# Chunked attention into a swish MLP on one core: the first two units' q and k transposed on TensorE instead of VectorE

## The chip, the core and the metric

The kernel runs on one core of a Trainium2 chip. Time is device time in microseconds (us) of one execution; lower is better. PE is TensorE (PEld its weight loads), DVE is VectorE, ACT is ScalarE, POOL is GpSimd, SP is SyncE. SBUF is the on-chip working memory, PSUM the eight banks that TensorE writes its results to.

## What is computed

Attention inside chunks of 64 tokens for 8 x 8 heads, then a two-layer MLP whose activation is h * sigmoid(beta * h):

```
q, k, v: (8, 8, 576, 64) float32        # batch, head, token, head_dim
scores = (q_chunk @ k_chunk.T) / 8      # 64 x 64 for each chunk and head
attn   = softmax(scores)
x      = (attn @ v_chunk) -> (4608, 512)
h      = x @ w_in                       # w_in (512, 2048)
out    = (h * sigmoid(beta * h)) @ w_out   # w_out (2048, 512), out (4608, 512) float32
```

## The kernel before

**Tiling.** The 4608 tokens are 18 units of 256 (four chunks, two tiles of 128 tokens, called s = 0 and s = 1). Two units make a block of 512 tokens. For a unit, the q and k rows are transposed so that the head dimension lies on the partitions; `emit_sc` writes the transposed scores into PSUM, ACT takes the exponential into `et`, `emit_pv` multiplies `et` with v (a column of ones beside v gives the sums), `emit_norm` divides on DVE and writes `x16`, and the result is transposed into `xt` (the products' right operand). For a block, `emit_m(j, m)` makes 128 rows of h (four matmuls), a tanh on ACT (`act`) and one DVE instruction (`vec`) that frees the product's PSUM bank and writes `gt`; `emit_t` multiplies `gt` with w_out, and ACT copies out.

**Order.** Everything is issued in the order of the code (`manual_schedule`), each engine in its own order. The part around the change is the start, written out by hand, before the first block's products run without a break. What waits there is filled on PE by matmuls whose result nobody reads (`emit_tiny`, `emit_idle`); one of them (L425) waits for a memset of `late` that stands in POOL's queue.

**Loads at the start.** SP loads q and k of heads 0 to 3 in float32 (`raw`), POOL loads heads 4 to 7 with a cast to float16 (`h`), both for 512 tokens with token 4p + r on partition p. Then POOL issues v of tiles 0 to 3 (`load_v`), writes the identity, and issues the eight pieces of w_in and the first of w_out. All of POOL's loads go through one queue.

**Units 0 and 1.** `emit_T_half(a)` handles four heads: for a = 0 ACT casts `raw` to float16 in 1 + 2 pieces, and DVE transposes q and k in 32 x 32 blocks, each pair of float16 values taken as one float32 word. The scores (`emit_sc_half`, L198) are therefore matmuls over 32 partitions, two (e = 0, 1) accumulated for each 64 x 64 result. The order that follows is: scores (0,0), exponential, scores (0,1), exponential, scores (1,0), `emit_pv(0)`, scores (1,1), the exponential of unit 1 in one piece, the two norms of unit 0, the transposes of `x16` of (0,0), `emit_pv(1)` for both tiles, the norms of (1,1) and (1,0), and then the products m = 0 to 3 over unit 0's 256 tokens with the remaining transposes between them:

```
d[0][0]()
emit_xt_pe(1, 1)
d[1][0]()
d.append(emit_m(0, 2, 0, 256, True))
d[0][1]()
emit_xt_pe(1, 0, nc.vector.tensor_copy)
```

`d[i][0]` is the tanh of product i, `d[i][1]` its DVE instruction. After these come products 0 to 3 over unit 1's tokens, then 4 to 15 over all 512. The pool `ps_p` has four PSUM banks, so the fifth product takes the bank of the first. `emit_xt_pe` transposes one 128 x 512 tile of `x16` on PE into PSUM (L303) and copies it to `xt` (L304), on ACT or, for (1,0), on DVE.

**Later.** `emit_T(2)` transposes unit 2 on DVE; its scores stand at position i = 8 of 16 in the first block's second layer, its `emit_pv` at i = 10, and unit 3's scores at i = 14.

Of the kernel before, what the change touches and what calls it, by code (L numbers as in the profile page):

```python
# [8 lines left out]
FP32 = mybir.dt.float32  # L9
FP16 = mybir.dt.float16  # L10
ACTF = mybir.ActivationFunctionType
# [4 lines left out]
def kernel(  # L16
# [10 lines left out]
    nc = tc.nc  # L27
# [5 lines left out]
    KFF = DFF // 128  # L33
    UNIT = 256
# [3 lines left out]
    scale = 1.0 / float(D) ** 0.5  # L38
# [20 lines left out]
    HH = H // 2  # L59
    raw0 = [const.tile([128, HH, 4, D], FP32, name=f"raw{i}") for i in range(2)]  # L60
    qk0 = [[const.tile([128, HH, 4, D], FP16, name=f"h0{i}{a}") for i in range(2)] for a in range(2)]
    qkT0 = [[const.tile([128, HH, 128, 2], FP16, name=f"t0{i}{a}") for i in range(2)] for a in range(2)]
    braw = const.tile([128, 32], FP32)
    gate = const.tile([128, 1], FP16)
    bt = const.tile([128, 32], FP32)
# [45 lines left out]
    def load_v(i):  # L111
        for off, n, b, s in runs(i * 128, 128):
            nc.gpsimd.dma_start(  # L113
                out=vbig[off:off + n, i, :, 0:D],
                in_=v[b, :, s:s + n, :].rearrange("h p d -> p h d"),
            )
# [54 lines left out]
    x16_t = {}  # L171
    xt_t = {}

    def emit_T_half(a):
        for i, h0, h1 in ((0, 0, HH), (1, 0, HH // 2), (1, HH // 2, HH)) if a == 0 else ((0, 0, HH), (1, 0, HH)):
            src = qk0[a][i][:, h0:h1]
            if a == 0:
                nc.scalar.copy(out=src, in_=raw0[i][:, h0:h1])  # L178
            nc.vector.transpose(  # L179
                out=qkT0[a][i][:, h0:h1].rearrange("p h s e -> p (h s e)").bitcast(FP32).rearrange(  # L180
                    "p (h i r) -> p h r i", h=h1 - h0, r=4),
                in_=src.rearrange("p h r d -> p (h r d)").bitcast(FP32).rearrange(
                    "p (h r i) -> p h r i", h=h1 - h0, r=4),
            )

    def emit_sc_half(u, a):
        if a == 0:
            et_t[u] = et_p.tile([128, 2, H, CH], FP16, tag="et", name="et")
            pool, tag = ((ps_s, "s"), (ps_x, "x"))[u]
            x_t["sc", u] = pool.tile([128, 2, H, CH], FP32, tag=tag, name="sc")  # L190
        sc = x_t["sc", u]
        qt, kt = qkT0[a]
        for h in range(HH):
            for e in range(2):
                for s in range(2):
                    p0 = 64 * u + 32 * s
                    for c in range(2):
                        nc.tensor.matmul(  # L198
                            out=sc[64 * c:64 * c + 64, s, HH * a + h, :],
                            lhsT=kt[p0:p0 + 32, h, 64 * c:64 * c + 64, e],  # L200
                            rhs=qt[p0:p0 + 32, h, 64 * c:64 * c + 64, e],
                            start=(e == 0),
                            stop=(e == 1),
                        )

    def emit_ex_half(u, a, n=1):
        hs = slice(HH * a, HH * (a + n))
        nc.scalar.activation(  # L208
            out=et_t[u][:, :, hs], in_=x_t["sc", u][:, :, hs], func=ACTF.Exp, scale=scale)

    ex_t = {}

# [38 lines left out]
        while ex_t[u] and not later:  # L251
            emit_ex(u)

    def emit_pv(u, where=("x", "s")):
        et = et_t.pop(u)
        for s in (1, 0) if u >= MU else (0, 1):
            i = 2 * u + s
            if where[s] == "p":
                x = [ps_p.tile([128, 4, 128], FP32, tag="p", name=f"y{r}") for r in range(2)]
            else:  # L260
                pool = {"x": ps_x, "s": ps_s}[where[s]]
                x = [pool.tile([128, 2, 4, 128], FP32, tag=where[s], name="x")]
            for g in range(4):
                for r in range(2):
                    for c in range(2):
                        nc.tensor.matmul(  # L266
                            out=(x[0][64 * c:64 * c + 64, r, g, 0:D + 1] if len(x) == 1 else
                                 x[r][64 * c:64 * c + 64, g, 0:D + 1]),
                            lhsT=(et[64 * r:64 * r + 64, s, 4 * c + g, :] if u < XU else
                                  et[64 * r:64 * r + 64, g % 2, 4 * s + 2 * c + g // 2, :]),  # L270
                            rhs=vbig[64 * r:64 * r + 64, i, 4 * c + g, 0:D + 1],
                        )
            x_t[u, s] = x
# [23 lines left out]

    def emit_xt_pe(u, s, copy=nc.scalar.copy):
        xf = x16_t.pop((u, s)).rearrange("p r h d -> p (r h d)")
        tag = "s" if u < 2 and (u, s) != (1, 0) else "xp"[s]  # L300
        xp = {"x": ps_x, "s": ps_s, "p": ps_p}[tag].tile([128, 4, 128], FP16, tag=tag, name="xp")
        for g in range(4):
            nc.tensor.transpose(out=xp[:, g, :], in_=xf[:, g * 128:(g + 1) * 128], identity=ident)  # L303
        copy(out=xt_at(u, s), in_=xp)  # L304
# [70 lines left out]
    def idle_bank():  # L375
        return ps_p.tile([128, 512], FP32, tag="p", name="warm")

    def emit_idle(n, w, d=None):
        d = idle_bank() if d is None else d
        for _ in range(n):  # L380
            nc.tensor.matmul(out=d[:, 0:w], lhsT=idle[:, 0:128], rhs=idle[:, 0:w])  # L381

    def emit_tiny(n):
        d = [ps_p.tile([128, 512], FP32, tag="p", name="tiny") for _ in range(2)]
        for i in range(n):
            c = i % 4
            p0, o0 = 32 * c, 64 * (c % 2)
            nc.tensor.matmul(
                out=d[c // 2][o0:o0 + 64, 0:8],
                lhsT=tiny[p0:p0 + 32, :],  # L390
                rhs=tiny[p0:p0 + 32, 0:8],
            )

    with tc.manual_schedule():
# [4 lines left out]
        for a, eng, dst in ((0, nc.sync, raw0), (1, nc.gpsimd, qk0[1])):  # L399
            for i, src in enumerate((q, k)):  # L400
                eng.dma_start(
                    out=dst[i],
                    in_=src[0, HH * a:HH * a + HH, 0:2 * UNIT, :].rearrange("h (p r) d -> p h r d", r=4),
                )
        bv = moe_beta.rearrange("(m w f) -> w m f", w=4, f=32)
        for w in range(4):
            nc.sync.dma_start(out=braw[32 * w:32 * w + KFF, :], in_=bv[w])
        for i in range(4):
            load_v(i)
            if i == 1:  # L410
                nc.gpsimd.memset(late, 0.0)
        nxt[0] = 2
        make_identity(nc, ident)
        for g in range(8):
            load_w_in(g)
        for g in range(3):
            load_w_out(g)
# [1 line left out]
        load_w_out(3)  # L419
        loads_to(3)  # L420

        emit_tiny(78)
        warm = idle_bank()
        emit_idle(3, 512, warm)
        nc.tensor.matmul(out=warm[:, 0:16], lhsT=idle[:, 0:128], rhs=late)  # L425
        emit_idle(8, 512, warm)
        emit_T_half(0)
        emit_sc_half(0, 0)
        emit_ex_half(0, 0)
        warm = idle_bank()  # L430
        emit_idle(6, 512, warm)
        emit_T_half(1)
        nc.vector.transpose(out=bt, in_=braw)
        emit_sc_half(0, 1)
        emit_ex_half(0, 1)
        emit_sc_half(1, 0)
        emit_idle(2, 512, warm)
        loads_to(5)
        emit_pv(0, ("s", "p"))
        emit_sc_half(1, 1)  # L440
        emit_ex_half(1, 0, 2)
        emit_norm(0, 0)
        emit_norm(0, 1)
        emit_idle(1, 512, warm)
        emit_idle(12, 64, warm)
        emit_xt_pe(0, 0)
        emit_pv(1, ("x", "p"))
        emit_norm(1, 1)
        emit_norm(1, 0)
        nc.scalar.activation(out=beta2, in_=bt[:, 0:KFF], func=ACTF.Copy, scale=0.5)  # L450
        emit_xt_pe(0, 1)
        d = [emit_m(0, m, 0, 256, True) for m in (0, 1)]
        d[0][0]()
        emit_xt_pe(1, 1)
        d[1][0]()
        d.append(emit_m(0, 2, 0, 256, True))
        d[0][1]()
        emit_xt_pe(1, 0, nc.vector.tensor_copy)
        d.append(emit_m(0, 3, 0, 256, True))
        for act, _ in d[2:]:  # L460
            act()
        for _, vec in d[1:]:
            vec()
        for m in range(4):
            emit_m(0, m, 256, 256)
# [1 line left out]
            emit_m(0, m)  # L467
        emit_T(2)
        for i in range(16):
            if i == 8:  # L470
                emit_sc(2)
            if i == 10:
                emit_pv(2)
                emit_norm(2, 0)
                emit_norm(2, 1)
                emit_T(3)
            if i == 13:
                emit_xt_pair(2)
            if i == 14:
                emit_sc(3, True)  # L480
            if i == 15:
                a0, v0 = emit_m(1, 0, 0, 256, True)
                a0()
                emit_pv(3)
                emit_norm(3, 0)
                emit_norm(3, 1)
                v0()
                emit_m(1, 1, 0, 256)
            emit_t(0, i % 4, 4 * (i // 4), 4 * (i // 4) + 4)
# [156 lines left out]
```

The softmax here doesn't subtract the row's maximum and nothing guards it: scores larger than these inputs give would overflow.

## Time and profile before

| | us |
|---|---|
| median of 9 runs (lowest, highest) | 287.75 (287.39, 288.11) |
| the profiled execution | 287.58 |
| span of its instructions | 285.7 |
| PE busy in it | 278.8 |
| DVE, ACT, POOL busy | 143.8, 146.2, 95.6 |
| PE busy in the first 17.17 us | 13.87 |

The span runs from the first to the last instruction; the profiled execution has 1.9 us around it. A row of the timeline gives the start, the length, engine, line, operation, output and inputs with shapes, the number of instructions merged into it, and in brackets the engine's idle time just before with what ended it. The length of a matmul counts its way through the array, so a stream is read from the starts.

### The profile page before, as it was taken

The numbers are of one execution on the slowest core, as the hardware profiler recorded it, in microseconds if no ns is written. First come the engines' busy times: TensorE is split into PE (matmuls) and PEld (weight loads), VectorE is DVE, ScalarE is ACT, GpSimd is POOL, SyncE is SP. The second block draws the span as 40 slices with busy tenths as digits, with TensorE's granted clock in tenths as the row PEclk, the third lists the DMA queues.
The fourth block names the chain that finished last, engine by engine and source line by source line (L and its number), as shares of the span: only waits on it lengthen the run. The fifth ranks groups of instructions, "written<-read, shape, count | busy, mean of one in ns | idle before, by whom it ended". The sixth has DMA issues, their size and how long they took to land.

```text
span 285.7 us, 6671 instructions
## 1 busy us (share of the span) xinstructions
PE 278.8 (98%) x2779; PEld 136.1 (48%) x2779; DVE 143.8 (50%) x268; ACT 146.2 (51%) x223; POOL 95.6 (33%) x125
## 2 busy tenths in 40 slices
PE   6999999999999999999999999999999999999995
PEld 3564456544544444444444444444444444444444
DVE  2777444776558453635463536363635463333301
ACT  4477128863567545455454545554545444444411
POOL 8843678498074981248617000000000000000000
PEclk9999999999999999999999999999999999999999
DMA  8999999999999999999999993425311221010012
GB/s 195 176 199 204 182 179 213 207 164 154 206 116 163 184 176 175 157 166 172 187 151 169 160 172 77 102 57 118 81 52 39 73 57 55 37 39 37 37 73 76
DMA packets 141085, 37.40 MB, mean 131 GB/s; under 512 B 128000, under 2 KB 136576, under 8 KB 141056
## 3 DMA queue, kind: packets, MB, share of 16 engines
q0 software_dynamic: 99136, 17.83, 79.8%
q1 hardware_dynamic: 41776, 19.09, 33.3%
q8 instruction: 22, 0.36, 0.5%
q10 hardware_dynamic: 144, 0.07, 0.1%
q14 instruction: 7, 0.06, 0.1%
HBM read 36.71 MB, written 9.44 MB: 162 GB/s over the span
## 4 chain that ended last, share of the span: by engine, by line
PE 94%; ACT 1%; DVE 1%; DMA 1%; issue 1%; DVEq 0%
PE hps L329 44%; PE ops L361 43%; PE x L266 2%; DMA raw<-in_q_dram 1%; PE sc L238 1%; PE ops L602 1%; PE sc L225 1%; DVE t L179 1%; PE y L266 1%; ACT xt L304 1%; PE xp L303 0%; PE sc L198 0%; ACT h L178 0%; ACT et L208 0%; PE warm L381 0%
## 5 line engine op out<-in xcount | busy, mean ns | idle before, releaser
L343 DVE SCALAR_TENSOR_TENSOR gt<-sg,hps 128x512 f16<-128x512 f32 (+1 forms) x153 | 99.2, 655 | 102.1 <-ACT sg L339 101.6
L329 PE MATMUL hps<-xt,win 128*128 128x512 f16 (+1 forms) x612 | 136.2, 367 | 1.0 <-ACT xt L304 0.7
L339 ACT ACTIVATE sg<-hps,beta 128x512 f32<-128x512 f32 (+1 forms) x153 | 100.3, 662 | 71.6 <-PE hps L329 70.0
L361 PE MATMUL ops<-wout,gt 128*128 128x512 f16 x560 | 131.1, 380 | 0.0
L329 PEld LDWEIGHTS <-win 128*128 128x128 f16 x612 | 58.1, 98 | 62.9 <-issue 1.5
L361 PEld LDWEIGHTS <-gt 128*128 128x128 f16 x560 | 54.1, 98 | 64.1
L371 ACT ACTIVATE osb<-ops 128x512 f32<-128x512 f32 x35 | 20.9, 598 | 42.7 <-PE ops L361 42.7
L113 POOL DMA_DIRECT2D vbig<-in_v_dram x40 | 34.0, 867 | 11.8 <-DMA wout<-in_moe_w_out_dram 3.7
L99 POOL DMA_DIRECT2D qu<-in_q_dram x22 | 18.7, 860 | 24.4 <-DMA qT<-qu 21.6
L287 DVE TENSOR_TENSOR x<-x,rd 128x512 f16<-128x512 f32 x27 | 18.7, 692 | 1.0
L99 POOL DMA_DIRECT2D ku<-in_k_dram x22 | 18.8, 876 | 0.6 <-DMA ku<-in_k_dram 0.3
L285 DVE RECIPROCAL rd<-x 128x8 f32<-128x8 f32 x27 | 5.4, 200 | 11.4 <-PE x L266 11.4
L247 ACT ACTIVATE et<-sc 128x1024 f16<-128x1024 f32 (+1 forms) x8 | 6.4, 811 | 8.8 <-PE sc L238 8.7
L231 ACT ACTIVATE et<-sc 128x1024 f16<-128x1024 f32 x10 | 10.2, 1021 | 0.8
L266 PEld LDWEIGHTS <-et 64*64 64x64 f16 x576 | 6.1, 107 | 7.4 <-issue 4.2
L287 DVE TENSOR_TENSOR x<-y,rd 128x256 f16<-128x256 f32 x18 | 7.6, 425 | 0.6
L105 POOL DMA_DIRECT2D qu<-in_q_dram x9 | 6.8, 768 | 2.6 <-DMA win<-in_moe_w_in_dram 1.2
L381 PE MATMUL warm<-idle 128*128 128x512 f16 (+1 forms) x32 | 7.5, 384 | 0.0
L105 POOL DMA_DIRECT2D ku<-in_k_dram x9 | 6.8, 760 | 1.9 <-DMA win<-in_moe_w_in_dram 1.3
L266 PE MATMUL x<-vbig,et 64*64 64x65 f16 x432 | 6.7, 194 | 0.2 <-ACT et L208 0.2
L614 DVE TENSOR_SCALAR osb<-ops 128x256 f32<-128x256 f32 (+1 forms) x2 | 0.7, 358 | 12.1 <-PE ops L602 12.1
L157 DVE STREAM_TRANSPOSE kT<-ku 128x512 f32<-128x512 f32 x6 | 4.2, 706 | 4.5 <-DMA ku<-in_k_dram 4.5
(46 smaller groups left out, 76.7 us busy)
## 6 DMA issues: line engine op xcount, KB each, us to landing
out_dram<-osb SPq DMA_DIRECT2D x35, 256.0 KB, 4.4
vbig<-in_v_dram POOLq DMA_DIRECT2D x32, 128.0 KB, 8.2
qu<-in_q_dram POOLq DMA_DIRECT2D x20, 128.0 KB, 6.5
ku<-in_k_dram POOLq DMA_DIRECT2D x20, 128.0 KB, 7.7
win<-in_moe_w_in_dram POOLq DMA_DIRECT2D x8, 256.0 KB, 9.1
wout<-in_moe_w_out_dram POOLq DMA_DIRECT2D x4, 512.0 KB, 12.8
qu<-in_q_dram POOLq DMA_DIRECT2D x3, 256.0 KB, 7.3
ku<-in_k_dram POOLq DMA_DIRECT2D x3, 256.0 KB, 7.8
```

The source lines that it names most:

```text
L99: nc.gpsimd.dma_start(out=tv[off:off + n, sp], in_=src[b, :, s:s + n, :].rearrange("h p d -> p h d"),)
L105: nc.gpsimd.dma_start(out=t[off // 2:(off + n) // 2], in_=src[b, :, s:s + n, :].rearrange("h (p r) d -> p h r d", r=2),)
L113: nc.gpsimd.dma_start(out=vbig[off:off + n, i, :, 0:D], in_=v[b, :, s:s + n, :].rearrange("h p d -> p h d"),)
L231: nc.scalar.activation(out=et, in_=sc, func=ACTF.Exp, scale=scale)
L266: nc.tensor.matmul(out=(x[0][64 * c:64 * c + 64, r, g, 0:D + 1] if len(x) == 1 else x[r][64 * c:64 * c + 64, g, 0:D + 1]), lhsT=(et[64 * r ...
L287: nc.vector.tensor_tensor(out=o, in0=z[..., 0:D], in1=rd[:, r].to_broadcast(list(o.shape)), op=ALU.mult)
L329: nc.tensor.matmul(out=hps[:, 0:n], lhsT=w_in16[m // 2][:, kk, (m % 2) * 128:(m % 2) * 128 + 128], rhs=xr[:, c0 // CH:(c0 + n) // CH, 2 * ...
L339: nc.scalar.activation(out=sg[:, 0:n], in_=hps[:, 0:n], func=ACTF.Tanh, scale=beta2[:, m:m + 1])
L343: nc.vector.scalar_tensor_tensor(out=gt_t[j][:, m, c0:c0 + n], in0=sg[:, 0:n], scalar=1.0, in1=hps[:, 0:n], op0=ALU.add, op1=ALU.mult,)
L361: nc.tensor.matmul(out=ops, lhsT=gt_t[j][:, kk, t * 128:(t + 1) * 128], rhs=w_out16[kk // 4][:, kk % 4, :], start=(kk == 0), stop=(kk == K ...
L371: nc.scalar.activation(out=osb, in_=ops, func=ACTF.Copy, scale=0.5)
L381: nc.tensor.matmul(out=d[:, 0:w], lhsT=idle[:, 0:128], rhs=idle[:, 0:w])
```

## The change

- q and k of units 0 and 1 are transposed on PE: 16 transposes of 128 x 64 for each of q and k and each half of the heads (a), into one PSUM bank for two heads, and one copy for each bank to SBUF, the first on ACT, the second on DVE. The copy reorders on the way (`p r t -> p t r`). The casts of `raw` are halved, one half on ACT, the other on DVE.
- A score is then one matmul over 64 partitions: 16 for each half and unit instead of 32.
- Order: both halves of the scores of both units come before `emit_pv(0)`; the tile s = 0 of `emit_pv(1)` moves ahead of the transposes of (0,1), the tile s = 1 behind products 0 and 1. All DVE instructions of products 0 to 3 (`vec`) come after the last copy to `xt`. The tanh's factor `beta2` is made earlier on ACT.
- POOL: the identity and piece 0 of w_in move forward, so v tiles 2 and 3 follow that piece; `late` follows v tile 0.
- The filler matmuls are counted anew: 11 around the L425 matmul become 7, and others are put between the steps.
- Unit 2's scores and its `emit_pv` stand one position later (i = 9 and 11).

```diff
+        make_identity(nc, ident)
...
-        for i in range(4):
-            load_v(i)
-            if i == 1:
-                nc.gpsimd.memset(late, 0.0)
+        load_v(0)
+        nc.gpsimd.memset(late, 0.0)
+        load_v(1)
+        load_w_in(0)
+        load_v(2)
+        load_v(3)
         nxt[0] = 2
-        make_identity(nc, ident)
-        for g in range(8):
+        for g in range(1, 8):
             load_w_in(g)
...
+    def emit_cast_half(i, f, cast):
+        hs = slice(2 * f, 2 * f + 2)
+        cast(out=qk0[0][i][:, hs], in_=raw0[i][:, hs])
+
+    def emit_T_half(a, i):
+        if (a, i) == (0, 0):
+            w = ps_x.tile([128, 2, 8, 128], FP16, tag="x", name="tq")
+            z = [w[:, f, 0:4] for f in range(2)]
+        else:
+            z = [ps_p.tile([128, 4, 128], FP16, tag="p", name="tq") for _ in range(2)]
+        tq_t[a, i] = z
+        for h in range(HH):
+            p0 = 64 * (h % 2)
+            for r in range(4):
+                nc.tensor.transpose(
+                    out=z[h // 2][p0:p0 + 64, r, :], in_=qk0[a][i][:, h, r, :], identity=ident)
+
+    def emit_cp_half(a, i, f, copy):
+        copy(
+            out=qkT0[a][i][:, f],
+            in_=tq_t[a, i][f].rearrange("p r t -> p t r"),
+        )
...
+        emit_tiny(75)
+        act_cp, vec_cp = nc.scalar.copy, nc.vector.tensor_copy
+        warm = idle_bank()
+        emit_idle(6, 512, warm)
+        nc.tensor.matmul(out=warm[:, 0:16], lhsT=idle[:, 0:128], rhs=late)
+        emit_idle(1, 512, warm)
+        for i in range(2):
+            emit_cast_half(i, 0, act_cp)
+            emit_cast_half(i, 1, vec_cp)
+        for i in range(2):
+            emit_T_half(0, i)
+            emit_cp_half(0, i, 0, act_cp)
+            emit_cp_half(0, i, 1, vec_cp)
+            if i == 0:
+                emit_idle(2, 512, warm)
+        emit_T_half(1, 0)
+        warm = idle_bank()
+        emit_sc_half(0, 0)
+        emit_ex_half(0, 0)
+        emit_sc_half(1, 0)
+        emit_cp_half(1, 0, 0, act_cp)
+        emit_cp_half(1, 0, 1, vec_cp)
+        emit_T_half(1, 1)
+        emit_cp_half(1, 1, 0, act_cp)
+        emit_cp_half(1, 1, 1, vec_cp)
         warm = idle_bank()
         emit_idle(3, 512, warm)
...
         nc.vector.transpose(out=bt, in_=braw)
         emit_sc_half(0, 1)
         emit_ex_half(0, 1)
-        emit_sc_half(1, 0)
-        emit_idle(2, 512, warm)
+        emit_sc_half(1, 1)
+        emit_ex_half(1, 0, 2)
+        nc.scalar.activation(out=beta2, in_=bt[:, 0:KFF], func=ACTF.Copy, scale=0.5)
+        emit_idle(3, 512, warm)
         loads_to(5)
         emit_pv(0, ("s", "p"))
...
         emit_norm(0, 0)
         emit_norm(0, 1)
-        emit_idle(1, 512, warm)
-        emit_idle(12, 64, warm)
+        emit_idle(3, 512, warm)
         emit_xt_pe(0, 0)
-        emit_pv(1, ("x", "p"))
-        emit_norm(1, 1)
+        emit_idle(15, 64, warm)
+        emit_pv(1, ("p", "x"), (0,))
         emit_norm(1, 0)
...
         emit_xt_pe(0, 1)
         d = [emit_m(0, m, 0, 256, True) for m in (0, 1)]
         d[0][0]()
-        emit_xt_pe(1, 1)
+        emit_pv(1, ("p", "x"), (1,))
+        emit_norm(1, 1)
         d[1][0]()
...
+        emit_xt_pe(1, 0)
+        d += [emit_m(0, m, 0, 256, True) for m in (2, 3)]
+        emit_xt_pe(1, 1, vec_cp)
         for act, _ in d[2:]:
             act()
-        for _, vec in d[1:]:
+        for _, vec in d:
             vec()
...
-            if i == 8:
+            if i == 9:
                 emit_sc(2)
-            if i == 10:
+            if i == 11:
                 emit_pv(2)
```

## The prediction

> **What bounds the kernel now.** I read the page's busy line first, then the table of two stretches (up to 17.17 us and after), then the timeline of the first 17.5 us engine by engine, and last the waits.
>
> ```profile
> PE 278.8 (98%) x2779; PEld 136.1 (48%) x2779; DVE 143.8 (50%) x268; ACT 146.2 (51%) x223; POOL 95.6 (33%) x125
> ...
> 0.00:17.17 17.17, 13.87 (x336) 8.24 (x336) 9.63 (x25) 8.48 (x14) 13.31 (x23) 1.00 1.38 187
> 17.17:285.70 268.53, 264.96 (x2444) 127.89 (x2444) 134.15 (x244) 137.72 (x210) 82.30 (x102) 1.00 1.12 127
> ```
>
> PE bounds it. After 17.17 us, PE's waits hold one entry of 0.2 us, so that stretch is a fixed 268.5 us of matmuls. The 17.17 us before hold waits, filler and 1.75 us of real products. The change acts there. It gains or loses what it moves the first product over unit 1, which starts at 17.17 and after which PE never stops.
>
> ```profile
> 4.85 3.23 PE L381 MATMUL warm<-idle 128*128 128x512 f16 x8
> ...
> 5.72 4.15 DVE L179 STREAM_TRANSPOSE t<-h 128x512 f32<-128x512 f32 x5 [3.28 <-ACT h L178]
> ...
> 8.38 1.47 PE L381 MATMUL warm<-idle 128*128 128x512 f16 x6
> ...
> 10.43 0.60 ACT L208 ACTIVATE et<-sc 128x512 f16<-128x512 f32 x1 [1.32 <-PE sc L198]
> ...
> 11.10 0.47 PEld L266 LDWEIGHTS <-et 64*64 64x64 f16 x32 [0.42 <-DMA vbig<-in_v_dram]
> ...
> 11.48 0.21 DVE L285 RECIPROCAL rd<-x 128x8 f32<-128x8 f32 x1 [1.58 <-PE x L266]
> ...
> 14.10 0.58 ACT L304 COPY xt<-xp 128x512 f16<-128x512 f16 x1 [0.36 <-PE xp L303]
> ...
> 14.73 1.03 PE L329 MATMUL hps<-xt,win 128*128 128x256 f16 x8 [0.67 <-ACT xt L304]
> ...
> 16.68 0.42 DVE L304 COPY xt<-xp 128x512 f16<-128x512 f16 x1 [0.33 <-PE xp L303]
> ...
> 17.03 1.14 DVE L343 SCALAR_TENSOR_TENSOR gt<-sg,hps 128x256 f16<-128x256 f32 x3
> ...
> 17.16 11.79 PEld L329 LDWEIGHTS <-win 128*128 128x128 f16 x64 [0.36 <-DVE xt L304]
> ```
>
> The reader is to see three marks. A = 11.10: unit 0's pv begins, as its exponential ends (11.03; v tile 0 had landed at 10.9). (Between: the scores that this exponential reads start at 9.93, and unit 0's two x16 are written at 12.42 and 13.51.) P = 14.73: the first product. U = 17.17: the first product over unit 1, behind the last copy to xt. A to P is 3.63 us, P to U 2.44.
>
> **The change part by part.** Sum: A moves, then A to P, then P to U.
>
> *q and k up to A.* Raw q lands at 4.6, raw k at 6.1, h of q at 7.4, h of k at 8.7 (issue plus landing time); nothing ahead of them moves. Removed: five DVE transposes (4.15 us, ending at 9.87). Added: casts in halves, on ACT 0.62 (row L178) at 4.64 and 6.13, on DVE beside them; 64 PE transposes; four copies on ACT, 0.58 (L304), four on DVE.
> A PE transpose: the 128x128 ones (L303) start every 55 ns. If the two column halves ran in pairs it would be half; if the weight load of 107 ns (L266, 64 columns) were not hidden, 107. I take 55, the nearest row: 0.88 for 16, and 0.2 until the result is there (the 128x128 ones last 0.22).
> A DVE copy: the row L304 says 0.425 for 128x512 float16 read in steps of one. [...] here the input steps over 128 elements. By the row A would be 11.6, [...]
> The chain: q transposes 5.29 to 6.17; ACT is held by the cast of k until 6.7, then copies to 7.25; DVE's copy waits for that one (same tile) and ends at 7.97. k transposes 6.78 to 7.66 (cast to 6.75), DVE copy 7.89 to 8.58. PE meanwhile does the transposes of (1,0) to 8.54; scores (0,0) and (1,0) from 8.68. Transposes (1,1) 8.95 to 9.83, DVE copy 10.05 to 10.75. Scores (0,1) at 10.79 instead of 9.93: the second half of k now takes 0.88 + 0.2 + 0.7 where one DVE transpose took 1.10. A score group of 16 matmuls reaches its reader in 0.375 (as pv, 11.10 to 11.48) where 32 took 0.51: exponential 11.16 to 11.76. A = 11.83, +0.73. v tiles 0 and 1 (10.9 and 11.3 in the trace) are there.
>
> *A to P.* Norms of unit 0 as before (2.41 to the last x16). Of its four transposes two no longer wait for the second half, -0.11: 3.52. P = 15.35, +0.62.
>
> *P to U.* In the trace both tiles of unit 1's pv are ahead of P and their norms run beside products 0 and 1. Now tile s = 1 stands behind these: 0.87 for eight products, 0.375 until the reciprocal, 0.94 until x16 is written (11.48 to 12.42), 0.585 to the copy's start (13.51 to 14.10). Then the copy, and behind it the `vec` of product 0, which frees the bank that unit 1's first product takes, and which used to stand ahead of the copy: 0.34 + 0.41 + 0.06 = 0.82. Sum 3.59 instead of 2.44: +1.15. Beside it PE has only transposes and products 2 and 3 (1.1 us). U = 18.94, **+1.77**.
>
> *What costs nothing, and its cover.* Identity (0.57 of POOL) ahead of v tile 0: v waits 8 us in the queue behind h of k anyway; without that cover v tiles 0 and 1 land 0.6 later, 11.5 and 11.9, at most 0.1 at A. v tiles 2 and 3 behind w_in piece 0: 256 KB take 1.3 (tile 3 at 12.7, piece 0 at 14.0), so piece 0 lands at 12.6 and the tiles at 13.2 and 14.0; they are read at 13.9 and 16.2. w_in 1 and all later loads keep their place. The three fillers before pv(0) (0.65) end 0.1 before the exponential does; the others lie in the norms. The L425 matmul: late is written about 4.4, PE comes at 4.65. `beta2` (0.23) falls in an ACT wait; SP's beta loads do not move. Unit 2 one position later: its transposes end at 35.96 and its pv was followed by three positions before `emit_xt_pair`, now two (1.73 + 0.38), and the norms need 2.15: no stall, 0.1 to spare. Unit 3's scores keep their place and the same work ahead; without the delay they would have 0.15 us to spare behind the DVE transposes that wait for k at 41.6.
>
> *PE's clock.* The granted clock reads 1.00 all along, but the fillers do not: eight take 3.23 from 4.85 (one each 0.43 to 7.4), six take 1.47 from 8.38 (0.22 each). The double rate came at about 7.6 us. [...] For it: now six run in a row from 2.1 to 4.6, where the trace has three and a hole of 1.25. If the double rate is there by 5.3, the sum is as above. If it comes at 7.6, the q transposes take 1.71, everything shifts and A is 12.7: U +2.6. [...] No row decides; I take the early one for the sum and keep the others for the range.
>
> **The rivals.**
> - Slow clock (above): 290.4[...]. For: the trace took 2.8 us of fillers in a row to rise. Against: the new first row lasts 3.0.
> - Faster: unit 1's exponential sets U. In the trace it starts at 12.12, pv(1) waits for it (0.24 at L266), and its norms follow; now it starts at 11.7 at the latest, and up to 0.65 earlier if the copies are short. If that wait decided, U would come 0.4 to 0.65 earlier: 287.1. It decides only if the last copy starts before 16.6, which needs tile s = 1 of pv(1) done by 14.6; the order puts it behind product 1, so P would have to be at 13.7 or before, and v tile 0 (10.9) + 3.52 is 14.4. Strongly against.
> - Not what it says: the transposes run in pairs and the copies at the short rate. Then scores (0,1) come at 10.1, A 11.15, U +1.1: 288.85. Even with A at v's landing (10.9) U is +0.8, 288.6: the floor of the forecast.
> - No change would need the P to U part to vanish and A to stay; nothing in the profile says so.
>
> **How the numbers follow.** The profiled execution took 287.58, 0.17 under the median of 287.75; the shift is added to the median: 287.75 + 1.77 = 289.5. Chances: the sum, with its paired and slow-copy forms (288.6 to 289.9), 0.55; double rate at 7.6 (290.0 to 290.8), 0.28; at 11 or later, 0.08; faster 0.05; within 0.2% 0.04. The measurement tells 0.2% (0.6 us) from no change at best. The range 288.5 to 290.9 leaves out the last three, 0.17.
>
> **What would show it.** Right: scores of the second half at 10.6 to 10.9, pv(0) at 11.6 to 11.9, products from 15.2 to 15.4, then a hole of about 0.9 us on PE before the first product over unit 1 at 18.9, that product waiting for DVE; DVE copies of 0.69; no PE wait behind it. Wrong in the clock: transposes starting every 107 ns. Wrong altogether: v tiles landing over 0.5 us elsewhere, or unit 1's first product at 17.2 or before.

## Result and the profile after

The changed kernel takes 289.75 us (median of 9 runs, 289.41 to 290.35), the kernel before 287.90 in the same comparison (29 runs). The medians are 1.85 us apart, where the prediction said +1.77 (289.5). The ratio of the runs is 1.0070, 95% interval 1.0061 to 1.0079, which is 1.8 to 2.3 us. The profiled execution after took 289.75 with a span of 288.0, so its span is 2.3 above that of before (285.7), whose profiled execution was a quick one (287.58 against its median of 287.90).

The busy line of the page, then the table of two stretches cut at the new U, 19.15 (columns: stretch, length, then busy time and instructions of PE, PEld, DVE, ACT, POOL, the granted clock, DMA share, GB/s):

```profile
PE 280.4 (97%) x2777; PEld 137.5 (48%) x2777; DVE 143.5 (50%) x269; ACT 147.4 (51%) x226; POOL 95.8 (33%) x125
...
0.00:19.15 19.15, 15.32 (x333) 9.36 (x334) 9.44 (x26) 9.74 (x17) 14.63 (x25) 1.00 1.39 189
19.15:288.00 268.85, 265.08 (x2444) 128.16 (x2444) 134.04 (x244) 137.66 (x209) 81.16 (x101) 1.00 1.11 126
```

Behind U stand the same 2444 matmuls as before; their stretch is 268.85 us long instead of 268.53. So 1.98 of the 2.3 us lie ahead of U, and 0.32 behind it. The timeline of the changed kernel up to U:

```profile
5.30 0.68 PE L190 MATMUL tq<-ident,h 128*64 128x128 f16 x16
...
9.44 1.07 ACT L194 COPY t<-tq 128x512 f16<-128x512 f16 x2
...
9.65 0.69 DVE L194 COPY t<-tq 128x512 f16<-128x512 f16 x1 [0.51 <-PE tq L190]
...
10.56 0.44 PE L211 MATMUL sc<-t,t 64*64 64x64 f16 x32 [0.20 <-ACT t L194]
...
11.69 0.22 PE L277 MATMUL x<-vbig,et 64*64 64x65 f16 x4
12.12 0.29 PE L277 MATMUL x<-vbig,et 64*64 64x65 f16 x12 [0.21 <-issue]
...
12.46 0.21 DVE L296 RECIPROCAL rd<-x 128x8 f32<-128x8 f32 x1 [2.00 <-PE x L277]
...
15.58 1.03 PE L340 MATMUL hps<-xt,win 128*128 128x256 f16 x8 [0.67 <-ACT xt L315]
...
18.34 0.42 DVE L315 COPY xt<-xp 128x512 f16<-128x512 f16 x1 [0.49 <-PE xp L314]
...
18.68 1.07 DVE L354 SCALAR_TENSOR_TENSOR gt<-sg,hps 128x256 f16<-128x256 f32 x3
...
19.15 0.61 PE L340 MATMUL hps<-xt,win 128*128 128x256 f16 x4 [0.85 <-DVE gt L354]
```

The three marks are read off directly: A = 11.69, P = 15.58, U = 19.15. Three things are to be seen besides. The scores of the second half (10.56) wait for ACT's second copy, which ends at 10.51, and not for DVE's, which ends at 10.34. Unit 0's pv starts at 11.69, does four matmuls, and then stands still until 12.12 with nothing named but "issue". And U waits 0.85 us for the `vec` of product 0, as the prediction had it.

The chain that ended last, between the first copies and pv(0), shows who sets A: DVE's copies of q and k in the first half, the first scores and their exponential, ACT's two copies in the second half, its scores, and then the three fillers.

```profile
7.26 1.30 DVE t L194 x2
...
8.60 0.32 PE sc L211 x12
...
8.95 0.60 ACT et L220
9.54 0.98 ACT t L194 x2
...
10.56 0.44 PE sc L211 x32
11.01 0.75 PE warm L392 x3
11.76 0.15 PE x L277 x4
```

A second stop like that of pv(0) is behind U, in the scores of unit 3. The first row is of before, the others are of the kernel after:

```profile
43.14 0.71 PE L238 MATMUL sc<-qT,kT 32*64 32x64 f16 x64
...
45.12 0.60 PE L249 MATMUL sc<-qT,kT 32*64 32x64 f16 x50
46.03 0.31 PE L249 MATMUL sc<-qT,kT 32*64 32x64 f16 x14 [0.31 <-issue]
```

64 score matmuls that belong together run as 50 and 14. The 0.31 us of idle time between them account for the 0.32 us by which the stretch behind U has grown.

| step | predicted | profile after |
|---|---|---|
| A | 11.10 + 0.73 = 11.83 | 11.69 (+0.59) |
| A to P | 3.52 (−0.11) | 3.89 (+0.26) |
| P to U | 3.59 (+1.15) | 3.57 (+1.13) |
| behind U | 0 | +0.32 |
| sum | +1.77 | +2.30 in one profile, +1.85 in the medians |

### The profile page after: what moved, and what is told of

Its sections match the earlier page's. It is cut to its first block, busy times and chain, and to the rows that moved or that the text cites. A ratio compares the mean times of both kernels' runs of the same rounds, so it can differ in the third digit from the quotient of the medians.

```text
span 288.0 us, 6669 instructions
## 1 busy us (share of the span) xinstructions
PE 280.4 (97%) x2777; PEld 137.5 (48%) x2777; DVE 143.5 (50%) x269; ACT 147.4 (51%) x226; POOL 95.8 (33%) x125
## 4 chain that ended last, share of the span: by engine, by line
PE 94%; DMA 2%; ACT 2%; DVE 1%; issue 1%; SPq 0%; DVEq 0%
PE hps L340 44%; PE ops L372 42%; PE x L277 2%; DMA raw<-in_k_dram 2%; PE sc L249 1%; PE ops L629 1%; PE sc L236 1%; PE y L277 1%; PE xp L314 1%; ACT xt L315 1%; ACT t L194 1%; DVE t L194 0%; PE warm L392 0%; PE sc L211 0%; DVE x L298 0%
## 5 line engine op out<-in xcount | busy, mean ns | idle before, releaser
L392 PE MATMUL warm<-idle 128*128 128x512 f16 (+1 forms) x33 | 6.9, 348 | 0.0
L641 DVE TENSOR_SCALAR osb<-ops 128x256 f32<-128x256 f32 (+1 forms) x2 | 0.7, 358 | 12.1 <-PE ops L629 12.1
L131 POOL DMA_DIRECT2D win<-in_moe_w_in_dram x8 | 6.0, 772 | 1.4 <-DMA win<-in_moe_w_in_dram 1.3
```

## Experiments

**1 to 4: the tail, the bank wait, and the fillers.** The first kernel is the one after, with both tiles of pv(1) ahead of the products again and the steps behind them as in before (the parts of the two tiles exchanged):

```diff
-        emit_pv(1, ("p", "x"), (0,))
+        emit_pv(1, ("p", "x"))
         emit_norm(1, 0)
+        emit_norm(1, 1)
         emit_xt_pe(0, 1)
         d = [emit_m(0, m, 0, 256, True) for m in (0, 1)]
         d[0][0]()
-        emit_pv(1, ("p", "x"), (1,))
-        emit_norm(1, 1)
-        d[1][0]()
         emit_xt_pe(1, 0)
-        d += [emit_m(0, m, 0, 256, True) for m in (2, 3)]
+        d[1][0]()
+        d.append(emit_m(0, 2, 0, 256, True))
+        d[0][1]()
         emit_xt_pe(1, 1, vec_cp)
+        d.append(emit_m(0, 3, 0, 256, True))
...
-        for _, vec in d:
+        for _, vec in d[1:]:
             vec()
```

> The changed kernel with the order of before from unit 1's pv on: both tiles of pv(1) ahead of the transposes of (0,1), the remaining transposes between products 1, 2 and 3, and vec of product 0 ahead of the last copy to xt. Theory (the tail from the first product to the first product over unit 1 costs 1.15 us because the norm of tile s = 1 stands behind products 0 and 1): that product starts at about 18.0 instead of 19.15, P to U is 2.4 to 2.5 us again, and the time falls by 1.1 us to about 288.7, still 0.7 to 0.9 above before. Rival (the loss is all in q and k ahead of pv(0), and the hole on PE would be there anyway): no change, 289.75.

Measured: 288.73 us, 1.0034 (1.0024 to 1.0044). Its timeline:

```profile
15.66 1.03 PE L340 MATMUL hps<-xt,win 128*128 128x256 f16 x8 [0.67 <-ACT xt L315]
...
16.75 0.60 PE L340 MATMUL hps<-xt,win 128*128 128x256 f16 x4
...
17.41 2.60 PE L340 MATMUL hps<-xt,win 128*128 128x256 f16 x20
17.62 0.42 DVE L315 COPY xt<-xp 128x512 f16<-128x512 f16 x1 [0.33 <-PE xp L314]
```

P is at 15.66, as in the kernel after (15.58). But product 3 now runs on into the first product over unit 1 (20 matmuls in one row from 17.41), whose copy to xt is done at 18.04. The weight load that waits for it starts at 18.09, so U is about 18.1 instead of 19.15, and P to U 2.4.

The second undoes only the bank wait: `vec` of product 0 ahead of the last copy.

```diff
+        d[0][1]()
         emit_xt_pe(1, 1, vec_cp)
...
-        for _, vec in d:
+        for _, vec in d[1:]:
             vec()
```

> The changed kernel with vec of product 0 alone put ahead of the last copy to xt. Theory (unit 1's first product waits for that instruction because it takes its PSUM bank): it starts 0.33 us earlier, at 18.8, then waiting for the copy, and the time falls by 0.3 us to about 289.4. Rival (the bank is not what it waits for): no change.

Measured: 289.36 us, 1.0057 (1.0040 to 1.0074). In its profile U is at 18.78, 3.25 behind P, and waits 0.52 for DVE's copy to xt.

The third makes the tail's change alone, in the kernel before: pv(1) one tile at a time, the second behind product 1, and `vec` of product 0 behind the last copy. (`emit_pv` takes the tile as a parameter for it, and the PSUM banks of the transposes follow the new order.)

```diff
...
-        emit_pv(1, ("x", "p"))
-        emit_norm(1, 1)
+        emit_pv(1, ("p", "x"), (0,))
         emit_norm(1, 0)
...
         d[0][0]()
-        emit_xt_pe(1, 1)
+        emit_pv(1, ("p", "x"), (1,))
+        emit_norm(1, 1)
         d[1][0]()
-        d.append(emit_m(0, 2, 0, 256, True))
-        d[0][1]()
-        emit_xt_pe(1, 0, nc.vector.tensor_copy)
-        d.append(emit_m(0, 3, 0, 256, True))
+        emit_xt_pe(1, 0)
+        d += [emit_m(0, m, 0, 256, True) for m in (2, 3)]
+        emit_xt_pe(1, 1, nc.vector.tensor_copy)
...
-        for _, vec in d[1:]:
+        for _, vec in d:
             vec()
```

> The kernel before with the changed kernel's order from unit 1's pv on (tile s = 1 behind products 0 and 1, all vec behind the last copy), q and k still transposed on DVE and all loads as before. Theory: P stays at 14.7, U comes at 18.3 instead of 17.17, +1.15 us: 289.0. Rival (the tail only costs together with the late v tiles or the PE transposes): no more than +0.2 us.

Measured: 288.93 us, 1.0036 (1.0023 to 1.0049), with P at 15.23 (h of q landed at 8.04 in this profile, 0.7 later than in before's, which moves A and P but not the tail) and

```profile
18.80 0.39 PE L329 MATMUL hps<-xt,win 128*128 128x256 f16 x2 [0.85 <-DVE gt L343]
```

U follows P by 3.57 us and waits 0.85 us for DVE, to the hundredth as in the kernel after. What follows from the three: the tail's reorder costs 1.04 us (0.36% of 287.9) where it is made alone, and 1.02 come back where it is undone (289.75 to 288.73). The bank wait is 0.3 of it by the profiles (P to U 3.57 in the kernel after, 3.25 in experiment 2); the medians fall by 0.39, but the two intervals overlap. With the tail undone 0.34% remain, about 1 us by the ratio and 0.83 by the medians. They belong to the rest of the change: what lies ahead of the tail, and the stop behind U.

The fourth takes fillers away: 2 instead of 6 ahead of the matmul on `late`.

```diff
-        emit_idle(6, 512, warm)
+        emit_idle(2, 512, warm)
         nc.tensor.matmul(out=warm[:, 0:16], lhsT=idle[:, 0:128], rhs=late)
```

> The changed kernel with 2 instead of 6 filler matmuls ahead of the one that waits for late, so that PE stands still from 2.9 to 4.6 us. Theory (TensorE's double rate comes from a row of about 3 us of matmuls, which the six fillers give): it comes at 7.5 us or later, transposes of q start every 53 ns instead of 28, the fillers behind them every 0.43 us, and U moves by 0.4 to 1.0 us: 290.2 to 290.8. Rival (the rate comes at a fixed time after the start, or the transposes bring it): fillers at 5.9 us are still 0.22 us apart and the time stays at 289.75.

Measured: 290.65 us, 1.0097 (1.0081 to 1.0114), 0.9 us above the kernel after; A is 12.56. The longer row of fillers earns its place. How PE's double rate (in before a wide filler every 0.22 us behind 7.6 us, every 0.43 ahead of it) depends on it was taken up next.

**5 to 8: the rate, the copies, ACT's order.** The fifth puts the longer row into the kernel before.

```diff
-        emit_idle(3, 512, warm)
+        emit_idle(6, 512, warm)
         nc.tensor.matmul(out=warm[:, 0:16], lhsT=idle[:, 0:128], rhs=late)
-        emit_idle(8, 512, warm)
+        emit_idle(7, 512, warm)
```

> The kernel before with 6 wide fillers ahead of the matmul on late and 7 behind it, instead of 3 and 8; nothing else. It asks whether the filler row alone moves the arrival of TensorE's double rate (7.6 us in the profile of before, 5.0 to 5.3 in that of after), and what that is worth where no transpose of q and k runs on PE. Theory (row sets the rate, but what ends last before A is DVE's transposes and ACT's exponential, so an earlier rate saves only the slow scores and pv): 287.6 to 287.9, the rate at 5 to 6 us in the profile, A at 10.9 to 11.1. Rival (the scores and pv at slow rate were on the path): 287.2 to 287.5. Rival (the row doesn't set the rate): 287.9, rate at 7 to 9 us.

Measured: 287.63 us, 0.9994 (0.9983 to 1.0005): no difference that can be told. Its filler rows on PE:

```profile
4.84 3.10 PE L381 MATMUL warm<-idle 128*128 128x512 f16 x7
...
8.26 1.47 PE L381 MATMUL warm<-idle 128*128 128x512 f16 x6
```

Seven fillers take 3.10 us, the next six 1.47. By the trace's record of the granted clock (more on it below) the double rate is there from 7.76 us, no sooner than in before (7.59), though the row runs unbroken from 2.1. In this profile, moreover, the second half of k lands at 9.41 instead of 8.75, which moves A to 11.75; the profile is not a picture of the median.

The sixth starts from the first kernel and makes q's copies read in steps of one, so that DVE copies at its short time; the strides move into the score matmuls' moving operand.

```diff
-    qkT0 = [[const.tile([128, 2, 128, 4], FP16, name=f"t0{i}{a}") for i in range(2)] for a in range(2)]
+    qkT0 = [[const.tile([128, 2, 4, 128] if i == 0 else [128, 2, 128, 4], FP16, name=f"t0{i}{a}") for i in range(2)] for a in range(2)]
...
-            in_=tq_t[a, i][f].rearrange("p r t -> p t r"),
+            in_=tq_t[a, i][f] if i == 0 else tq_t[a, i][f].rearrange("p r t -> p t r"),
...
-        qt, kt = (z.rearrange("p g t r -> p g (t r)") for z in qkT0[a])
+        qt = qkT0[a][0].rearrange("p g r t -> p g t r")
+        kt = qkT0[a][1].rearrange("p g t r -> p g (t r)")
...
-                            rhs=qt[64 * par:64 * par + 64, g, t0:t0 + 64],
+                            rhs=qt[64 * par:64 * par + 64, g, t0 // 4:t0 // 4 + 16],
```

> The kernel after with both tiles of pv(1) ahead of the products, as in the first run of this study (288.73, 1.0034), and with q's copies out of the transposes' banks in steps of one; the strides go to the moving operand of the scores, k's copies stay as they are. It asks whether DVE's slow copies (0.69 instead of 0.43 us) are on the path to A. Theory (ACT's order of exponential and copies releases the second half's scores, DVE's q copies are beside it): DVE's q copies 0.43, but 288.6 to 288.8, no gain over the first run. Rival (DVE's 0.69 is on the path, as the prediction had it): 0.25 less, 288.4 to 288.5. Rival (the strided moving operand makes the score matmuls slower): above 288.9.

Measured: 289.12 us, 1.0054 (1.0034 to 1.0075). Its timeline shows both times of the same operation in one kernel, q's copy and k's:

```profile
7.31 0.42 DVE L194 COPY t<-tq 128x512 f16<-128x512 f16 x1 [0.71 <-ACT t L194]
...
10.52 0.69 DVE L194 COPY t<-tq 128x512 f16<-128x512 f16 x1 [1.31 <-PE tq L190]
```

The short copy is real, 0.27 us less each. What it is worth can't be read from the time, because the strided moving operand costs more than that. The scores of the second half, first in this kernel, then in the first one, both at the full clock:

```profile
11.16 1.06 PE L212 MATMUL sc<-t,t 64*64 64x64 f16 x32
...
10.87 0.45 PE L211 MATMUL sc<-t,t 64*64 64x64 f16 x32 [0.20 <-ACT t L194]
```

So the last of the three expectations came true, and A is 12.90 here against 12.00 in the first kernel. Whether DVE's copies are on the path is not settled by this run. In the chain of the kernel after, two of them are.

The seventh, also from the first kernel, lets ACT do the copies of q's second half ahead of unit 0's first exponential.

```diff
-        emit_ex_half(0, 0)
         emit_sc_half(1, 0)
         emit_cp_half(1, 0, 0, act_cp)
         emit_cp_half(1, 0, 1, vec_cp)
+        emit_ex_half(0, 0)
```

> The kernel after with both tiles of pv(1) ahead of the products, and with unit 1's first score half and the two copies of q's second half ahead of unit 0's first exponential on ACT's queue. Theory (scores (0,1) wait for ACT's last copy, which stands behind the exponential of 0.6 us): A 0.3 to 0.45 us earlier than in the first run of this study, time 288.3 to 288.4 (ratio 1.0013 to 1.0018). Rival (A is set by DVE's copy of k, as the prediction had it, 0.17 us ahead of ACT's): gain at most 0.2, 288.5 to 288.7. Rival (the exponential of the first half, moved behind, becomes late itself): no gain, 288.7 or more.

Measured: 288.65 us, 1.0036 (1.0026 to 1.0047), against 288.73 and 1.0034 without: no gain. Yet the exponential did come earlier. PE's row in its profile:

```profile
11.50 0.22 PE L277 MATMUL x<-vbig,et 64*64 64x65 f16 x4
12.13 0.29 PE L277 MATMUL x<-vbig,et 64*64 64x65 f16 x12 [0.41 <-issue]
```

A moved to 11.50, and the stop behind the fourth matmul grew: it lasts until 12.13, and in the kernel after it ended at 12.12. PE stays at one instruction until 12.1 in both, though the data is 0.19 us earlier here. The theory that ACT's order sets the end was right about A, and the end is set elsewhere.

The eighth takes away all fillers between 2.06 us and pv(0), leaving PE with transposes and scores.

```diff
-        emit_idle(6, 512, warm)
         nc.tensor.matmul(out=warm[:, 0:16], lhsT=idle[:, 0:128], rhs=late)
-        emit_idle(1, 512, warm)
...
-            if i == 0:
-                emit_idle(2, 512, warm)
...
-        emit_idle(3, 512, warm)
         nc.vector.transpose(out=bt, in_=braw)
...
-        emit_idle(3, 512, warm)
         loads_to(5)
```

> The kernel after without any of its fillers between 2.06 us and pv(0) (6, 1, 2, 3 and 3 taken out; the matmul on late stays). PE then has only the transposes of q and k and the scores in this stretch. It asks whether PE transposes bring the double rate. Theory (they count as work): the rate arrives about 3 us after the first dense stretch, at 9 to 12 us, time 290.5 to 291.2. Rival (transposes do not count): the rate comes only with the scores and pv, at 13 us or later, all transposes at half rate, A over 13.2, time 291.5 to 293. Rival (fillers are no cause of anything): 289.8, as the kernel after.

Measured: 290.38 us, 1.0102 (1.0069 to 1.0136), with single times from 289.42 to 293.14. The profiled execution is the longest of them. In it PE is still slow behind pv(0),

```profile
12.81 1.46 PE L392 MATMUL warm<-idle 128*128 128x512 f16 x3
```

three fillers in 1.46 us, and by the clock's record the double rate comes only at 21.18.

**9 to 12: the stop.** The trace holds a queue of instructions: 22 packets and 0.36 MB, that is 16 KB each.

```profile
q8 instruction: 22, 0.36, 0.5%
```

In the kernel after, one of them starts at 9.90, 2.22 us ahead of the stop's end; in the seventh kernel one starts at 9.78, 2.35 ahead. The weight loads and matmuls that PE has begun when it stops can be counted: they are the numbers behind the x of PE and PEld in the table of stretches, here from 0 to the stop and from 0 to the stop in unit 3's scores, for the kernel after and for the seventh.

```profile
0.00:12.10 12.10, 9.97 (x223) 5.57 (x224) 4.69 (x11) 6.32 (x10) 10.51 (x19) 1.00 1.30 187
0.00:46.00 46.00, 41.89 (x607) 22.72 (x607) 24.56 (x52) 23.27 (x38) 31.18 (x46) 1.00 1.55 188
```

```profile
0.00:12.10 12.10, 10.00 (x223) 5.65 (x224) 4.71 (x11) 6.60 (x10) 10.50 (x19) 1.00 1.30 188
0.00:44.70 44.70, 41.63 (x607) 22.77 (x607) 24.63 (x52) 23.06 (x38) 29.69 (x44) 1.00 1.53 189
```

Both stop behind 447 and behind 1214 instructions. With the two and three other instructions of PE's stream ahead of them (a drain and semaphore instructions) that is place 449 and 1217, 768 or three times 256 apart. The packets fit: in the kernel after, the one at 9.90 is the first of its queue, and the fourth starts at 43.60, 2.43 us ahead of 46.03, so three packets for 768 instructions. So the stop looked like the edge of a block of 256 instructions that has not come yet, which is an inference from these counts. That can be tested by moving the program against the count. The 8-column matmuls at the start run at four in 53 ns, so 32 of them (0.43 us) can be exchanged for one wide filler of the slow rate without moving anything in time, while the count moves by 62. The ninth kernel has more of them:

```diff
-        emit_tiny(75)
+        emit_tiny(107)
...
-        emit_idle(6, 512, warm)
+        emit_idle(5, 512, warm)
         nc.tensor.matmul(out=warm[:, 0:16], lhsT=idle[:, 0:128], rhs=late)
```

> The kernel after with 32 more of the 8-column matmuls at the start (107 instead of 75, 0.43 us in all) and one wide filler of 0.43 us less behind them: PE's row has the same length, and all that follows stands 62 PE instructions later in PE's stream. In the profile of after, pv(0) stops for 0.41 us at the 449th PE instruction, and unit 3's scores for 0.50 at the 1217th, 768 = 3 x 256 further, each 2.2 to 2.4 us after a packet of 16 KB on the instruction queue began. Theory (the stops are instruction blocks of 256 that come late): neither stop is at its old instruction; none in pv(0), whose 32 matmuls then run in one row with the reciprocal 0.38 after A; a stop of up to 0.6 us at the 1217th again, which now is 62 instructions earlier in the program, in the same scores of unit 3. Time 289.2 to 289.5 (0.3 to 0.5 less than after). Rival (a wait of pv(0) itself, for v or for a bank): the stop stays at pv(0)'s fifth matmul, 289.75.

Measured: 290.01 us, 1.0079 (1.0063 to 1.0094), which can't be told from the kernel after: the place of the stop was forecast rightly, the gain was not. pv(0) runs without a stop (12.43 to the reciprocal at 12.81, 0.38). A stop has appeared in the four transposes behind pv(1)'s second tile, and the count there, up to 17.50, is 703, which is 447 and 256:

```profile
17.14 0.64 PE L314 MATMUL xp<-ident,x 128*128 128x128 f16 x4
...
0.00:17.50 17.50, 14.20 (x351) 8.82 (x352) 8.01 (x22) 8.78 (x15) 13.51 (x23) 1.00 1.39 188
```

Four transposes take 0.40 in the kernel after and 0.64 here. But A is 12.43, since the second half of q and k landed late:

```profile
8.62 0.66 PE L190 MATMUL tq<-ident,h 128*64 128x128 f16 x16 [1.13 <-DMA h<-in_q_dram]
```

h of q lands at 8.58 here and at 7.27 in the kernel after. The instruction packet that started at 9.90 there starts at 5.54 here, in the middle of that transfer. The DMA view of 5.50 to 5.60 has it as

```profile
q8 instruction: 1, 0.02, 70.9%
```

which is 0.709 x 16 engines x 0.1 us, or 1.13 us of one DMA engine. That the packet held up one engine's part of h is an inference. In part it may be chance, since h of q also lands at 8.03 to 8.05 in three other profiles (experiments 3, 5 and 12) that have no packet there.

The tenth does the same to the seventh kernel.

> The kernel after with both tiles of pv(1) ahead of the products and ACT's copies of the second half ahead of the first exponential (288.65 in this study), and with the same 32 tiny matmuls more and one filler less. That kernel's profile stops at pv(0)'s fifth matmul for 0.61 us, until 12.13, although the exponential is 0.2 us earlier than in after. Theory (late instruction block): the stop is gone, reciprocal at 11.9 instead of 12.47, U 0.4 to 0.6 earlier, 288.0 to 288.3, so within 0.2 per cent of before or just outside. Rival (the stop is pv(0)'s own): 288.65. Rival (something else, v tile 1 or unit 1's exponential, is late next and takes the gain): 288.4 to 288.6.

Measured: 289.06 us, 1.0047 (1.0032 to 1.0063), so no better than the 288.65 it started from. Again no stop in pv(0) (12.13, reciprocal at 12.50), again a packet early (5.30) and h of q late (8.26), and again a stop of 0.34 us behind 703 instructions, at 17.03. In this profile the stop in pv(0) is gone, and a later load has taken its gain.

The eleventh is the eighth kernel again.

> A second look at the kernel after without fillers between 2.06 us and pv(0), whose first profile fell on its longest run (293.14, the others 289.4 to 290.7): TensorE's double rate came there only at about 20 us. Theory (the start of the rate falls differently from run to run, and transposes and scores count as work): this profile is near 290.3, and the rate comes at 9 to 12 us. Rival (transposes do not count): rate at 13 us or later again, 291.5 or more.

Measured: 289.70 us in one run. By the clock's record the double rate comes at 10.93 here, against 21.18 in experiment 8.

The twelfth moves the count the other way.

```diff
-        emit_tiny(75)
+        emit_tiny(43)
...
-        emit_idle(6, 512, warm)
+        emit_idle(7, 512, warm)
         nc.tensor.matmul(out=warm[:, 0:16], lhsT=idle[:, 0:128], rhs=late)
```

> The kernel after with 32 fewer of the 8-column matmuls at the start (43) and one wide filler more (7 ahead of the matmul on late): all that follows stands 62 PE instructions earlier in PE's stream. Theory (instruction blocks of 256): no stop inside pv(0), whose last instruction is then ahead of the 449th; the 449th is among the four transposes of unit 0's first tile (13.45 in the profile of after), which stop for 0 to 0.9 us; the other stop is 62 instructions later in the program, in unit 3's or unit 2's pv at 47.7. Time 289.3 to 290.4. Rival (the stop is pv(0)'s own): it stays at the fifth matmul of pv(0), 289.75.

Measured: 289.53 us, 1.0066 (1.0048 to 1.0083); the profiled execution is the longest of the six, 290.34. PE's row and the count up to the stop:

```profile
11.99 0.32 PE L277 MATMUL x<-vbig,et 64*64 64x65 f16 x16
12.15 0.29 PE L277 MATMUL y<-vbig,et 64*64 64x65 f16 x16
...
14.41 0.38 PE L314 MATMUL xp<-ident,x 128*128 128x128 f16 x4 [1.21 <-DVE x L298]
...
0.00:14.30 14.30, 11.11 (x223) 5.94 (x224) 6.56 (x17) 6.77 (x11) 12.06 (x21) 1.00 1.39 186
```

pv(0) runs through, and PE now stops ahead of the first tile's transposes, behind 447 instructions once more. The row puts this down to DVE, but x is written at 13.30 (12.61 and 0.69), 1.1 us before. A packet of instructions started at 12.13, 2.28 ahead of 14.41. With the count moved by 62 in either direction the stop has stayed behind 447 instructions, or 256 more, and left the operation at which it stood. It is no wait of pv(0), for v or for a bank.

**The granted clock in these traces.** The 1.00 in the rows hides the rise. Each trace has a record of the granted clock whose first entry is the rise itself, and time without an entry counts as full in the rows. By the record the full clock begins at 5.12 us in the kernel after, at 7.59 in before, and in experiments 1, 4, 5, 8 and 11 at 7.71, 10.40, 7.76, 21.18 and 10.93. PE's pace changes there: in experiment 1 the pairs of transposes start 108 ns apart up to 7.70 and 56 ns apart from 7.79 on.

In the fourteen traces a stretch of full clock lasts 283.306, 279.893, 276.480 or 269.653 us. These lengths differ by 3.413 us or twice that. From the lengths alone comes an estimate of the author's, that the clock changed only at edges 3.413 us apart, which lie differently in each execution; the edges themselves are not shown. By it the step ahead of the rise began at 1.71 in the kernel after, and PE was busy for all of its 3.41 us. In experiment 1, with the same fillers, an edge lay at 4.29; PE was busy ahead of it too, but for 1.2 us with 8-column matmuls, and the clock rose one step later, at 7.71.

In the last 3.41 us ahead of the rise in experiments 4 and 11, PE was busy at least 0.97 of the time, most of it with transposes. Of these alone (L190; columns: stretch, length, then busy time and instructions of PE and PEld), experiment 4 and then 11:

```profile
6.99:10.40 3.41, 2.64 (x46) 2.40 (x48) 1.00 1.95 179
...
7.52:10.93 3.41, 2.81 (x48) 2.33 (x45) 1.00 1.94 176
```

So in these two traces the clock rose behind 3.41 us that held 2.64 and 2.81 us of transposes. What decides it is open: in experiment 8 the stretch from 7.52 to 10.94, with PE busy 2.96 of 3.42 us, was followed by no rise, while in before one followed 2.77 of 3.41 us with fillers (4.18 to 7.59).

## Why the prediction was right, and where it was not

- **P to U.** The largest term, +1.15, came out at +1.13, by the mechanism named: tile s = 1 of pv(1) behind two products, then the bank that `vec` of product 0 frees. Experiments 1 and 3 put 1.0 us on it from both sides, and experiment 2 puts 0.3 of that on the bank.
- **A, +0.73: the step that failed is the pace of a transpose and who ends last in the second half.** The first half went as said: DVE's two copies end at 8.55 (said: 8.58), on the path, and the transposes of (1,1) start at 8.95. DVE's 0.69, the author's estimate with the 0.69 of the 512-element L287 beside it, was right: a copy takes 0.69 with strides and 0.42 without in experiment 6. But the 55 ns of the 128x128 transposes were taken, and these transposes start in pairs, 13 ns apart: in the kernel after the sixteen of q start within 0.46 us, about 30 ns each, close to the lower bound of the prediction. So DVE's last copy ends at 10.34, not at 10.75, and ACT ends last instead: unit 0's first exponential (8.95 to 9.54) stands between its copies, and its last copy ends at 10.51. The three fillers ahead of pv(0), which were to end before the exponential (11.53), end behind it: A is 0.16 later than that end, and only 0.05 later in experiments 8 and 11, which have no such fillers. Misses of opposite sign left +0.59.
- **A to P, −0.11: wrong by 0.37.** The norms and transposes between took what was said (12.46 to 15.58 is 3.12; 11.48 to 14.73 was 3.25 before). From A to the reciprocal it was to be 0.375, as before, and is 0.77. The difference is the stop inside pv(0), 0.41 us between two starts, behind 447 instructions. The prediction had no such stop. In experiments 7, 9, 10 and 12 a stop stood behind 447 instructions or behind 703, whatever the operation there.
- **Behind U, 0: wrong by 0.32.** It is the stop 768 instructions further on, in unit 3's scores, where the same order of work had been costed at nothing.
- **The clock.** "Early by 5.3 us" held in the profile of the kernel after (5.12). It is no property of the program: with the same row of six fillers the rate came at 7.71 in experiment 1 and at 7.76 in experiment 5. It matters less than the prediction's +2.6 for 7.6 us, for two reasons. At the slow rate the sixteen transposes of q start within 0.76 us, 51 ns each and not 107, so A is 12.00 in experiment 1 and not 12.7. And the stop held PE until 12.12 in the kernel after anyway: the reciprocal starts at 12.46 in both. In experiments 4 and 11 the clock rose at 10.40 and 10.93, behind 3.41 us of which 2.64 and 2.81 were transposes.
- **The rivals.** "Not what it says" was half true: the transposes were paired, the copies were not short. The faster case, that unit 1's exponential sets U, did not occur. One sign that was named as wrong altogether did: v tiles 0 and 1 landed at 9.6 and 10.5, not at 10.9 and 11.3, but early, and nothing waits for them. That 289.5 lies so near 289.75 is in part luck: the mis-sized terms ahead of U (−0.14 and +0.37) partly cancelled, and the profile's +2.30 is more than the medians' +1.85.

No kernel here is faster than the kernel before. That kernel with six fillers is level with it, and the best of the changed ones, with the tail put back, are at 1.0034 (experiment 1) and 1.0036 (experiment 7, with ACT's copies first).

What stays open: what sets the start of a packet of instructions (9.9 us here, 8.7 in before, 5.3 to 5.5 with 32 matmuls more, 12.1 with 32 fewer), how much of h's late landing is the packet's doing, and what work makes the clock rise. The moved loads, the halved casts and the later place of unit 2 were not tried alone.

## What to carry to other kernels

A change that moves work behind the first products pays for the whole chain that now follows them (norm, transpose, copy, bank), and that chain can be added up from rows of the trace (here 3.59 us against 3.57). When an engine stops in the middle of a row of equal instructions with "issue" as the only releaser, count its instructions up to there. Here two such stops stood 768 apart, and when the program was shifted by 62 instructions they stayed at their number or came 256 later; that speaks for instructions that come late, and data 0.19 us earlier did not remove the stop (A at 11.50 instead of 11.69 in experiment 7). An engine named as the releaser that had long been done can be the same sign (in experiment 12 DVE, done 1.1 us before).

## What the hardware did that was not expected

- PE stopped at fixed counts of its instructions: behind 447 and 1214 weight loads and matmuls in the kernel after and in experiment 7, behind 703 in 9 and 10, behind 447 in 12. In PE's whole stream that is 256 or three times 256 apart, and in the kernel after the first and the fourth of the 16 KB packets stand ahead of the two stops. That one packet brings 256 instructions is an inference from this. The first instruction behind the stop started 2.22 and 2.43 us after its packet did in the kernel after, 2.35 in experiment 7 and 2.28 in experiment 12, while a row of 32 weight loads and 32 matmuls of 64x64 is through in 0.45 us. The stops inside rows were 0.41 and 0.50 us long from start to start in the kernel after and 0.61 in pv(0) of experiment 7.
- A packet of instructions took 0.97 us of one DMA engine in the kernel after (the one at 9.90) and 1.13 us in experiment 9, while the loads ran.
- The arrival of the double rate varied between two executions of one kernel by 10.25 us (10.93 in experiment 11, 21.18 in experiment 8), with a granted clock of 1.00 in the rows throughout. The stretches of full clock differ by 3.413 us or twice that.
- 64x64 scores whose moving operand is strided took 1.06 us for 32 in experiment 6, against 0.45 us without strides in experiment 1.
- h of q landed at 7.4 us in before, at 7.27 in the kernel after, at 8.03 to 8.05 in experiments 3, 5 and 12, at 8.26 in experiment 10 and at 8.58 in experiment 9, from kernels that issue it at the same time (1.24 to 1.25 us in before and after).
